# Keys into their slot, transposed in place, and half of wq kept on the chip: two attention and feed-forward layers at decode

## The chip, the core and the metric

The kernel runs on one core of a Trainium2 chip. The metric is the device time of the program in microseconds (us). The engines are called by their short names: PE is TensorE, DVE VectorE, ACT ScalarE, POOL GpSimd, and SP is the engine that issues the loads here. "PEld" is the loading of a weight into the matrix array, which overlaps the products.

## The reference, cut to what matters

One token for each of 8 sequences goes through the same pair of blocks twice: attention over a cache, then a feed-forward network, each behind a layer norm and added to the residual.

```python
B, Sq, D = 8, 1, 512;  Hq, Hkv, Sk, Dh = 32, 8, 8192, 128;  F = 1792
def A(x):                       # x is normalized
    q = (x @ wq)                # 512 x 4096, 32 heads of 128
    scores = q . k * Dh**-0.5   # 4 query heads share one of 8 key heads
    p = softmax(scores)         # over 8192 positions
    return (p @ v) @ wo         # 4096 x 512
def Bf(x):
    return silu(x @ w1) @ w2
x = x + A(norm(x));  x = x + Bf(norm(x))
x = x + A(norm(x));  x = x + Bf(norm(x))
```

All data are bf16. The two caches hold 134 MB each (8 sequences x 8 heads x 8192 x 128), and both layers read them. The kernel reads the keys once, because a sequence's keys stay on the chip from the first layer to the second, and reads the values twice.

## The kernel before

**Units and passes.** The work is cut into units: one layer, one sequence b, one key head g, that is 128 units. There are nine passes (the loop at L909). Pass b = -1 has the eight first-layer units of sequence 0. Pass b = 0 to 6 mixes the second layer of sequence b with the first layer of sequence b+1, alternating; pass 7 has the second layer of the last sequence alone. The second layer of a sequence can start when all its first-layer units have gone through the output projection, the feed-forward block and the next norm. To have something to do over that chain, the values of the last `N_DEF` = 3 second-layer units of a pass are held back and done at the beginning of the next pass (`held`).

**One unit.** `keys` makes p: `expand` (L651) and `spread` (L658) lay the four query heads out as a block-diagonal weight `bd`; `score` (L673) does 64 products, each with 128 columns of keys as the weight; then come the maximum over the unit (`mx` on DVE, `mall` on POOL), the subtraction, the exponential on ACT, a rearrangement through PE (`swap`, L708) and the copy back, with sum and reciprocal beside it. `values` (L755) does 64 products with V as the weight. For a first-layer unit the result goes on through `out_proj_a` with its piece of wo.

**Keys.** In the first layer a head of keys (2 MB) arrives in two halves in the ring (`load_k`, L375). `turns` (L617) transposes it in four pieces with DVE's transpose of 32 x 32 blocks of 32-bit words (two bf16 at a time) from the ring into the head's slot in `kts`, which has eight slots of 2 MB. The second layer of the same sequence uses the slot again; the next sequence's transposes wait for its scores (`scored`). On the way the transposes also set the order of words in a row: from (c4, f, j) to (f, c4, i), so that the 128 columns of one weight lie 4 bytes apart (L674).

**The ring.** `ring` has `N_CELL` = 11 cells of 0.5 MB. Halves of keys and of V take two neighbouring cells, a quarter of half of wq one, a head's piece of wo one. `queries` (L569) loads its half of wq as four cells in every pass, for the first norm and for each sequence; all four have to be there before its products start, and all four are given back after them.

**The order of the work.** All loads are issued by SP, one after the other in the order in which the program lists them (`advance` puts the keys of a unit ahead of the V of the unit before it). SP waits in front of a load until what it overwrites has been read, and everything behind it waits too. What each engine does in which order, and which ring cell a load takes, is settled beforehand by a planner (`Plan`, L134): it steps through the program with fixed durations for each piece of work (for example `T_TURN` for a transpose) and serves, on each engine, the ready piece with the lowest priority number. On the chip each engine then runs its list strictly in order.

**Norms.** `norm_nodes` (L395) sums x and its squares over the partitions with products (L404, L409), makes mean and variance with three small DVE operations (L415, L420, L428), the inverse root on POOL (L433), and applies them (L438). `ffn_nodes` (L456) follows with up, tanh, gate and down. w1 and w2 stay on the chip; `load_ffn` (L864) loads them in the middle of the first pass (L942).

Of the kernel before, what the change touches and what calls it, by code (L numbers as in the profile page):

```python
# [7 lines left out]
DH = 128  # L8
SM_SCALE = DH ** -0.5
LN_EPS = 1e-5  # L10

N_CELL = 11
N_SC = 3
N_P = 3
N_DEF = 3
N_OT = 2
N_BD = 2
T_TURN = 1.2
# [115 lines left out]
class Plan:  # L134
# [3 lines left out]
    RATE = {1: 2.57, 2: 2.51}  # L138
    LAND = 2.0
    HOP = 0.07  # L140
# [107 lines left out]
def _build(ctx, nc, A_x, A_k_cache, A_v_cache, A_wq, A_wo, B_w1, B_w2, out):  # L248
# [22 lines left out]
    kts = sb([128, G * SLOT], BF16, "kts")  # L271
    w1_sb = sb([128, KT, F], BF16, "w1")
    w2_sb = sb([128, FT, D], BF16, "w2")
    ident = sb([128, 128], BF16, "ident")
    ones = sb([128, 1], BF16, "ones")
    sel = sb([128, 4, 4, 32], BF16, "sel")
    sel2 = sb([128, 4, 4, 32], BF16, "sel2")
    mask = sb([128, 4], BF16, "mask")
    expo = sb([128, 8], FP32, "expo")
# [6 lines left out]
    negm = sb([128, 8], FP32, "negm")  # L286
# [18 lines left out]
    ksem = [DmaCounter(syn.new_sem(f"kt{i}")) for i in range(2)]  # L305
    rsem = [DmaCounter(syn.new_sem(f"ring{i}")) for i in range(N_CELL)]
    wsem = {n: DmaCounter(syn.new_sem(f"w_{n}")) for n in ("w1", "w2", "x")}
# [67 lines left out]
    def load_k(b, g, half):  # L375
        src = A_k_cache[b, g].rearrange("(p hh y) d -> hh p (y d)", p=128, hh=2)
        return load_cells(f"k{b}.{g}.{half}", 2, [(lambda buf: buf, src[half])])
# [17 lines left out]
    def norm_nodes(tag, prio, b0, nb, deps):  # L395

        st = MI[:, 480:480 + nb]
# [3 lines left out]
        def stats():  # L401
            steps = []
            for kt in range(KT):
                steps.append(lambda kt=kt: pe.matmul(  # L404
                    st, ones[:, 0:1].to_broadcast([128, 128]), xs[:, bs, kt], start=(kt == 0), stop=(kt == KT - 1)))
            for j in range(nb):
                for kt in range(KT):
                    col = xs[:, b0 + j, kt:kt + 1]
                    steps.append(lambda kt=kt, j=j, col=col: pe.matmul(  # L409
                        sq[:, j:j + 1], col.to_broadcast([128, 128]), col,  # L410
                        start=(kt == 0), stop=(kt == KT - 1)))
            mms(steps, reads=[res("ones"), res("xs")], writes=[res("misc")])

        def mean():
            op(dve, lambda: dve.tensor_scalar(negm[:, 0:nb], st, -1.0 / D, None, op0=ALU.mult),  # L415
               reads=[res("misc")], writes=[res("negm")])

        def vari():
            if nb == 1:
                op(dve, lambda: dve.tensor_scalar(  # L420
                    var[:, 0:1], st, negm[:, 0:1], sq, op0=ALU.mult, op1=ALU.add),
                    reads=[res("misc"), res("negm")], writes=[res("var")])
            else:
                op(dve, lambda: dve.tensor_tensor(var[:, 0:nb], st, negm[:, 0:nb], ALU.mult),
                   reads=[res("misc"), res("negm")], writes=[res("var")])
                op(dve, lambda: dve.tensor_tensor(var[:, 0:nb], sq, var[:, 0:nb], ALU.add),
                   reads=[res("misc"), res("var")], writes=[res("var")])
            op(dve, lambda: dve.tensor_scalar(  # L428
                var[:, 0:nb], var[:, 0:nb], 1.0 / D, LN_EPS, op0=ALU.mult, op1=ALU.add),
                reads=[res("var")], writes=[res("var")])  # L430
# [5 lines left out]
        def apply():  # L436
            if nb == 1:
                op(dve, lambda: dve.tensor_scalar(  # L438
                    xn[:, b0, :], xs[:, b0, :], negm[:, 0:1], rstd[:, 0:1], op0=ALU.add, op1=ALU.mult),
                    reads=[res("xs"), res("negm"), res("rstd")], writes=[res("xn")])  # L440
            else:
                nm = negm[:, 0:nb].unsqueeze(2).to_broadcast([128, nb, KT])
                rs = rstd[:, 0:nb].unsqueeze(2).to_broadcast([128, nb, KT])
                op(dve, lambda: dve.tensor_tensor(big_x, xs[:, bs, :], nm, ALU.add),
                   reads=[res("xs"), res("negm")], writes=[res("ring", 1)])
                op(dve, lambda: dve.tensor_tensor(xn[:, bs, :], big_x, rs, ALU.mult),
                   reads=[res("ring", 1), res("rstd")], writes=[res("xn")])

        a = plan.add(f"{tag}.stats", "PE", 0.3 + 0.2 * nb, stats, prio, deps)
        m = plan.add(f"{tag}.mean", "DVE", 0.18, mean, prio, [a])  # L450
        v = plan.add(f"{tag}.var", "DVE", 0.45, vari, prio, [m])
        r = plan.add(f"{tag}.root", "POOL", 0.6, root, prio, [v])
# [53 lines left out]
    st6 = negm[0:NB, 0:6]  # L506
# [3 lines left out]
    def consts():  # L510
        op(pool, lambda: pool.memset(ones[:, :], 1.0), writes=[res("ones")])
# [4 lines left out]
        iv = ident[:, :].rearrange("p (f j e) -> p f e j", f=2, e=2)  # L516
        sv = sel[:, :, :, :].rearrange("p (f e) a j -> p f e a j", f=2)
        for a in range(4):
            op(pool, lambda a=a: pool.tensor_copy(sv[:, :, :, a, :], iv), reads=[res("ident")], writes=[res("sel")])
            op(pool, lambda a=a: pool.tensor_copy(  # L520
                sel2[:, :, a, :], ident[:, :].rearrange("p (dd j) -> p j dd", j=4)),
                reads=[res("ident")], writes=[res("sel2")])
        op(pool, lambda: pool.memset(expo[:, :], -0.5), writes=[res("expo")])
# [7 lines left out]
    def first_norm():  # L531
        op(dve, lambda: dve.bn_stats(st6, xr), reads=[last], writes=[res("negm")])
        op(dve, lambda: dve.bn_aggr(mv, st6), reads=[res("negm")], writes=[res("var")])
        op(dve, lambda: dve.tensor_scalar(mv[:, 1:2], mv[:, 1:2], LN_EPS, None, op0=ALU.add),
           reads=[res("var")], writes=[res("var")])
# [28 lines left out]
    f4 = plan.add("f.turn", "PE", 0.5, first_turn, -5, [f3])  # L564
# [4 lines left out]
    def queries(tag, prio, half, b0, nb, deps):  # L569

        wn = [load_wq(half, kt) for kt in range(KT)]
        out_n = {}
        last = []
        for g0, g1 in ((4 * half, 4 * half + 1), (4 * half + 1, 4 * half + 4)):
# [3 lines left out]
            def mul(g0=g0, nh=nh, qp=qp):  # L578
                steps = []
                for h in range(nh):  # L580
                    c = (R * g0 + h) * DH - GR * half
                    for kt in range(KT):
                        steps.append(lambda h=h, kt=kt, c=c: pe.matmul(  # L583
                            qp[:, h * nb:(h + 1) * nb], gran(wn[kt].give)[:, c:c + DH], xn[:, b0:b0 + nb, kt],
                            start=(kt == 0), stop=(kt == KT - 1)))
                mms(steps, reads=[r for w in wn for r in cells_of(w)] + [res("xn")], writes=[res("misc")])

            def copy(g0=g0, g1=g1, qp=qp):
                hd = slice(R * g0, R * g1)
                if nb == 1:  # L590
                    op(dve, lambda: dve.tensor_copy(qtb[:, hd], qp), reads=[res("misc")],
                       writes=[res("qtb", g) for g in range(g0, g1)])
                else:
                    op(dve, lambda: dve.tensor_copy(qab[:, :, hd], qp.rearrange("p (h b) -> p b h", b=nb)),
                       reads=[res("misc")], writes=[res("qab", g) for g in range(g0, g1)])

            m = plan.add(f"{tag}.q{g0}", "PE", 0.5 * (g1 - g0), mul, prio, wn + deps + last)
            last = [plan.add(f"{tag}.qc{g0}", "DVE", 0.17, copy, prio, [m])]
            for g in range(g0, g1):
                out_n[g] = last[0]  # L600
        for w in wn:
            frees(m, w)
        return out_n

# [12 lines left out]
    def turns(b, g):  # L617

        tn = []
        new = slot(g).bitcast(U32).rearrange("p (q ck f c4 i) -> p q ck c4 f i", q=4, f=2, i=32, c4=4)  # L620
        for half in range(2):
            kn = load_k(b, g, half)
            for c in range(2):
                def turn(kn=kn, c=c, q=2 * half + c):
                    raw = gran(kn.give, 2).bitcast(U32).rearrange(
                        "p (q ck c4 f j) -> p q ck c4 f j", q=2, c4=4, f=2, j=32)
                    op(dve, lambda: dve.transpose(new[:, q], raw[:, c]), reads=cells_of(kn),  # L627
                       writes=[res("kt", g)], add=(q > 0))
                tn.append(plan.add(f"t{b}.{g}.{2 * half + c}", "DVE", T_TURN, turn, count[0] + 0.5,
                                   [kn] + scored.get(g, []) + tn[-1:]))  # L630
            frees(tn[-1], kn)
        kept[b, g] = tn

    def keys(layer, b, g, q_dep, late=None):
# [3 lines left out]
        pr = u  # L638
# [33 lines left out]
        for q in range(4):  # L672
            def score(q=q):  # L673
                kv = slot(g).rearrange("p (ck f n e) -> p ck f e n", f=2, ck=NCG, e=2)  # L674
# [80 lines left out]
    def values(h, wo=None):  # L755
# [34 lines left out]
        else:  # L790
# [6 lines left out]
            def spread():  # L797
                steps = [lambda j=j: pe.matmul(  # L798
                    ot[:, 8 + R * j:8 + R * j + R], sel2[:, j].rearrange("p a k -> p (a k)"), attna[:, hd],
                    start=True, stop=True) for j in range(R)]  # L800
                mms(steps, reads=[res("sel2"), res("attna", g)], writes=[res("ot", o)])
# [78 lines left out]
    def load_wo_all():  # L880
        for i in range(2):
            n = plan.load(f"woall{i}", 4, None, scored[2 * i], ring=False)

            def emit(i=i):
                dma(sp, slot(2 * i).rearrange("p (h d) -> p h d", h=16), wo_v[:, 16 * i:16 * i + 16, :], ksem[i],
# [23 lines left out]
    for b in range(-1, NB):  # L909
        ready = None  # L910
        prio = count[0] - 4
        if b >= 0:
# [4 lines left out]
            for k, h in enumerate(held):  # L917
                if k == 1:
                    second_q.update(queries(f"c{b}", prio, 0, b, 1, [ready]))
                values(h)  # L920
                ends.append(h)
# [4 lines left out]
        def advance(unit):  # L926
            while unit not in made:
                k = todo.pop(0)
                layer, kb, g = k
                if layer == 0:  # L930
                    turns(kb, g)
                    if kb == 0 and g % 4 == 0:
                        first_q.update(queries("f", count[0] - 5, g // 4, 0, NB, [f5]))
                    made[k] = keys(0, kb, g, first_q[g])
                else:
                    if g % 4 == 0 and g >= (4 if held else 0):
# [83 lines left out]
```

## Time and profile before

| what | value |
|---|---|
| median of 3 runs | 1231.23 us (1230.66 to 1232.52) |
| the profiled execution | 1229.31 us |
| its span, from the first to the last instruction | 1227.8 us |
| busy: PE, PEld, DVE, ACT, POOL | 56%, 51%, 44%, 9%, 10% |
| bytes moved, mean rate over the span | 485.00 MB, 395 GB/s |
| V loads, each from issue to landing (median) | 256 of 1 MB, 10.0 us |
| key loads | 128 of 1 MB, 10.1 us |
| wq loads | 72 of 0.5 MB, 11.0 us |
| wo loads | 64 of 0.5 MB, 10.4 us; at the end 2 of 2 MB, 16.5 us |
| transposes of keys (L627) | 256, 310.8 us of DVE |
| products with V (L775), products of the scores (L678) | 8192 of each |

The page cuts the span into 40 slices and gives, for each, the busy share of every engine and the rate of the transfers. A row of a group reads: line, engine, operation, out<-in, shapes, count | busy us, mean ns of one | idle time of the engine just before them, and what ended it. The time of a load from issue to landing includes the loads queued ahead of it. A window's row has its bounds, its length, busy us and count for PE, PEld, DVE, ACT and POOL, the granted clock, the busy share of the transfers, and GB/s.

### The profile page before, as it was taken

How to read it: one execution, taken by the hardware profiler on the slowest of the kernel's cores; microseconds unless marked ns; L12 is line 12 of the kernel's file. 1: busy time of each engine (PE TensorE's matmuls, PEld its weight loads, DVE VectorE, ACT ScalarE, POOL GpSimd, SP SyncE). 2: the span in 40 equal slices, each digit the busy share in tenths (PEclk: the TensorE clock that was granted, in tenths of full speed). 3: DMA queues.
4: the chain of work that ended last, by engine and by line, in shares of the span. 5: the costliest groups of instructions: out<-in, count | busy, mean ns of one | idle time of the engine just before them, and what ended most of it. 6: DMA issues, size and time to landing. Idle time of an engine off the chain costs nothing.

```text
span 1227.8 us, 48979 instructions
## 1 busy us (share of the span) xinstructions
PE 683.5 (56%) x22688; PEld 627.0 (51%) x22688; DVE 536.5 (44%) x1236; ACT 108.9 (9%) x330; POOL 117.1 (10%) x295
## 2 busy tenths in 40 slices
PE   3334656565565655646556564656556555565665
PEld 2333545465454654546455464545545455454554
DVE  5533445614364254633446334461536515454221
ACT  0000000101011010100101000010101100011000
POOL 1000100101011010101001010010101101010110
DMA  9999699999999999999999999999999999999994
GB/s 371 416 405 417 272 403 419 416 390 417 409 417 408 385 419 416 415 404 367 417 399 417 415 393 417 406 403 373 420 416 403 412 368 408 412 417 401 383 370 186
DMA packets 81580, 485.00 MB, mean 395 GB/s; under 512 B 8400, under 2 KB 14304, under 8 KB 32224
## 3 DMA queue, kind: packets, MB, share of 16 engines
q1 hardware_dynamic: 81376, 481.87, 96.8%
q8 instruction: 178, 2.92, 0.9%
q14 instruction: 26, 0.21, 0.0%
HBM read 481.83 MB, written 0.01 MB: 392 GB/s over the span
## 4 chain that ended last, share of the span: by engine, by line
DMA 40%; issue 21%; PE 18%; DVE 15%; POOL 2%; SPq 2%; ACT 1%; POOLq 0%; DVEq 0%
DMA ring<-in_A_v_cache_dram 28%; DVE kts L627 9%; DMA ring<-in_A_k_cache_dram 9%; PE ot L775 6%; PE sc L678 5%; DMA ring<-in_A_wq_dram 3%; SPq L327 2%; PE misc L583 2%; DVE sc L700 2%; DVE small L690 1%; PE misc L485 1%; PE misc L467 1%; POOL small L695 1%; PE sc L715 1%; DVE small L725 1%
## 5 line engine op out<-in xcount | busy, mean ns | idle before, releaser
L775 PE MATMUL ot<-p,ring 128*128 128x4 bf16 x8192 | 283.2, 167 | 241.1 <-DMA ring<-in_A_v_cache_dram 202.1
L775 PEld LDWEIGHTS ot<-p,ring 128*128 128x128 bf16 x8192 | 252.7, 104 | 260.7 <-DMA ring<-in_A_v_cache_dram 214.6
L627 DVE STREAM_TRANSPOSE kts<-ring 128x1024 uint32<-128x1024 uint32 x256 | 310.8, 1228 | 43.7 <-DMA ring<-in_A_k_cache_dram 43.1
L678 PE MATMUL sc<-bd,kts 128*128 128x16 bf16 x8192 | 275.6, 175 | 88.1 <-issue 59.0
L678 PEld LDWEIGHTS sc<-bd,kts 128*128 128x128 bf16 x8192 | 247.9, 104 | 99.3 <-issue 64.5
L690 DVE TENSOR_REDUCE small<-sc 128x4 f32<-128x256 f32 x128 | 53.9, 421 | 237.5 <-PE sc L678 237.5
L695 POOL PARTITION_ALL_REDUCE small<-small x128 | 47.6, 372 | 726.1 <-DVE small L690 681.8
L705 ACT ACTIVATE expd<-sc 128x256 bf16<-128x256 f32 x128 | 48.9, 382 | 556.8 <-DVE sc L700 550.8
L715 PE MATMUL sc<-expd,ident 128*32 128x64 bf16 x2048 | 54.0, 239 | 48.1 <-ACT expd L705 35.7
L730 POOL PARTITION_ALL_REDUCE small<-small x128 | 55.0, 430 | 236.1 <-DVE small L725 202.2
L700 DVE TENSOR_TENSOR sc<-sc,small 128x256 f32<-128x256 f32 x128 | 54.0, 422 | 31.6 <-POOL small L695 31.6
L583 PE MATMUL misc<-xn,ring 128*128 128x1 bf16 (+1 forms) x1152 | 36.5, 166 | 49.6 <-DMA ring<-in_A_wq_dram 32.0
L725 DVE TENSOR_REDUCE small<-expd 128x4 f32<-128x256 bf16 x128 | 51.2, 400 | 23.0 <-ACT expd L705 23.0
L715 PEld LDWEIGHTS sc<-expd,ident 128*32 128x32 bf16 x2048 | 31.9, 118 | 56.7 <-ACT expd L705 43.3
L583 PEld LDWEIGHTS misc<-xn,ring 128*128 128x128 bf16 x1152 | 33.9, 104 | 52.3 <-issue 48.1
L721 ACT ACTIVATE p<-sc 128x256 bf16<-128x256 f32 x128 | 49.0, 383 | 114.7 <-PE sc L715 114.7
L827 PE MATMUL yt<-z,ring 128*128 128x4 bf16 x1024 | 37.0, 167 | 39.5 <-DVE z L805 26.6
L827 PEld LDWEIGHTS yt<-z,ring 128*128 128x128 bf16 x1024 | 32.9, 104 | 44.2 <-issue 43.0
L805 DVE TENSOR_TENSOR z<-ot,small 128x16 bf16<-128x16 f32 x64 | 10.5, 164 | 82.4 <-PE ot L798 82.4
L794 ACT ACTIVATE attna<-ot 128x4 bf16<-128x4 f32 x64 | 11.1, 173 | 362.8 <-PE ot L775 362.8
L786 DVE TENSOR_TENSOR qab<-ot,small 128x4 bf16<-128x4 f32 x64 | 10.2, 160 | 74.0 <-PE ot L775 74.0
L662 DVE TENSOR_TENSOR bd<-qx,mask 128x64 bf16<-128x64 f32 x128 | 27.6, 216 | 19.4 <-PE qx L654 19.4
(64 smaller groups left out, 250.4 us busy)
## 6 DMA issues: line engine op xcount, KB each, us to landing
ring<-in_A_v_cache_dram SPq DMA_DIRECT2D x256, 1024.0 KB, 10.0
ring<-in_A_k_cache_dram SPq DMA_DIRECT2D x128, 1024.0 KB, 10.1
ring<-in_A_wq_dram SPq DMA_DIRECT2D x72, 512.0 KB, 11.0
ring<-in_A_wo_dram SPq DMA_DIRECT2D x64, 512.0 KB, 10.4
kts<-in_A_wo_dram SPq DMA_DIRECT2D x2, 2048.0 KB, 16.5
w<-in_B_w_dram SPq DMA_DIRECT2D x2, 1792.0 KB, 15.3
ring<-in_A_x_dram SPq DMA_DIRECT2D x1, 8.0 KB
out_dram<-ring SPq DMA_DIRECT2D x1, 8.0 KB
```

Source lines behind the costliest of these rows:

```text
L583: steps.append(lambda h=h, kt=kt, c=c: pe.matmul(qp[:, h * nb:(h + 1) * nb], gran(wn[kt].give)[:, c:c + DH], xn[:, b0:b0 + nb, kt], start= ...
L627: op(dve, lambda: dve.transpose(new[:, q], raw[:, c]), reads=cells_of(kn), writes=[res("kt", g)], add=(q > 0))
L678: steps.append(lambda cg=cg, fe=fe: pe.matmul(sc[:, 16 * cg:16 * cg + 16], kv[:, cg, fe // 2, fe % 2], bd[:, 16 * fe:16 * fe + 16], start= ...
L690: op(dve, lambda: dve.tensor_reduce(mxp[sm], sv.rearrange("p (k h) -> p h k", h=R), AX.X, ALU.max), reads=[res(*scr)], writes=[res("mxp", ...
L695: op(pool, lambda: pool.partition_all_reduce(mxa[sm], mxp[sm], 128, bass.bass_isa.ReduceOp.max), reads=[res("mxp", sm)], writes=[res("mxa" ...
L700: op(dve, lambda: dve.tensor_tensor(v, v, mxa[sm].unsqueeze(1).to_broadcast([128, NCH, R]), ALU.subtract), reads=[res("mxa", sm)], writes= ...
L715: steps.append(lambda c4=c4, P=P: pe.matmul(new[32 * P:32 * P + 32, c4], ident[:, 32 * c4:32 * c4 + 32], src[:, P], start=True, stop=True))
L721: op(act, lambda: act.activation(pt[:, :], sc[:, 256:512], ACT.Copy), reads=[res(*scr)], writes=[res("p", sm)])
L725: op(dve, lambda: dve.tensor_reduce(ssm[sm], pe_out[:, :].rearrange("p (k h) -> p h k", h=R), AX.X, ALU.add), reads=[res("expd")], writes= ...
L730: op(pool, lambda: pool.partition_all_reduce(ssa[sm], ssm[sm], 128, bass.bass_isa.ReduceOp.add), reads=[res("ssm", sm)], writes=[res("ssa" ...
L775: steps.append(lambda x=x, k=k: pe.matmul(ot[:, 0:R], vt[:, x, :], pt[:, k:k + R], start=(P == 0 and x == 0), stop=(P == 3 and x == NCG - 1)))
L827: steps.append(lambda j=j, dt=dt: pe.matmul(YT[:, dt * R:(dt + 1) * R], w[:, j, dt * 128:(dt + 1) * 128], zt[:, R * j:R * j + R], start=(g ...
```

## The change

Keys are no longer loaded into the ring. One load of 2 MB per head goes straight to the slot in `kts`, and waits there for the scores of the slot's last user. The four transposes work in place: each takes words 8 bytes apart (f is now the innermost index of a row), 1024 words of each partition, and writes the transposed block where it read it. All of them wait for the whole head. The 128 columns of a score weight then lie 8 bytes apart.

The ring shrinks from 11 to 7 cells. In the room that this frees, `wq0`, half of wq (the queries of heads 0 to 3) stays on the chip; it is loaded once. The other half still comes through the ring in every pass, but its four cells are used and given back one by one (`queries_1`). `N_DEF` goes from 3 to 4. Keys are listed two units ahead instead of one, except at the start of a pass. `load_ffn` moves from the middle of the first pass to its end. The work of the chain between passes gets the lowest priority numbers (`FIRST`). In the norm, the sums give the negative mean directly (weights of -1/D), eps is added by two products, the squares use x/D made by ACT, and two small DVE operations go. `sel2` is dropped, since `sel` now has its layout. Some of the planner's durations change too.

```diff
-N_CELL = 11
+N_CELL = 7
-N_DEF = 3
+N_DEF = 4
-T_TURN = 1.2
+T_TURN = 1.23
+FIRST = -1000000
...
-    RATE = {1: 2.57, 2: 2.51}
+    RATE = {1: 2.57, 2: 2.51, 4: 2.48}
-    HOP = 0.07
+    HOP = 0.1
...
+    wq0 = sb([128, KT, GR], BF16, "wq0")
...
-    def load_k(b, g, half):
-        src = A_k_cache[b, g].rearrange("(p hh y) d -> hh p (y d)", p=128, hh=2)
-        return load_cells(f"k{b}.{g}.{half}", 2, [(lambda buf: buf, src[half])])
+    def load_k(b, g):
+        n = plan.load(f"k{b}.{g}", 4, lambda: dma(
+            sp, slot(g), A_k_cache[b, g].rearrange("(p y) d -> p (y d)", p=128), ksem[g], writes=[res("kt", g)]),
+            scored.get(g, []), ring=False)
+        return n
...
     def turns(b, g):
+        kn = load_k(b, g)
         tn = []
-        new = slot(g).bitcast(U32).rearrange("p (q ck f c4 i) -> p q ck c4 f i", q=4, f=2, i=32, c4=4)
-        for half in range(2):
-            kn = load_k(b, g, half)
-            for c in range(2):
-                def turn(kn=kn, c=c, q=2 * half + c):
-                    raw = gran(kn.give, 2).bitcast(U32).rearrange(
-                        "p (q ck c4 f j) -> p q ck c4 f j", q=2, c4=4, f=2, j=32)
-                    op(dve, lambda: dve.transpose(new[:, q], raw[:, c]), reads=cells_of(kn),
-                       writes=[res("kt", g)], add=(q > 0))
+        for q in range(4):
+            def turn(q=q):
+                v = slot(g).bitcast(U32).rearrange("p (q n f) -> p q f n", q=4, f=2)[:, q]
+                op(dve, lambda: dve.transpose(v, v), reads=[], writes=[res("kt", g)], add=(q > 0))
...
-                kv = slot(g).rearrange("p (ck f n e) -> p ck f e n", f=2, ck=NCG, e=2)
+                kv = slot(g).rearrange("p (ck n f e) -> p ck f e n", f=2, ck=NCG, e=2)
...
+    def queries_1(tag, prio, b0, nb, deps):
+        qp = MI[:, 0:16 * nb]
+        last = []
+        for kt in range(KT):
+            wn = load_wq(1, kt)
+            def mul(kt=kt, wn=wn):
+                ...
+            last = [plan.add(f"{tag}.r{kt}", "PE", 0.5, mul, prio, [wn] + deps + last)]
+            frees(last[0], wn)
...
-            for k, h in enumerate(held):
-                if k == 1:
-                    second_q.update(queries(f"c{b}", prio, 0, b, 1, [ready]))
+            second_q.update(queries_0(f"c{b}", prio, b, 1, [ready]))
+            for h in held:
                 values(h)
...
-            advance(vs[min(i + 1, len(vs) - 1)])
-            if b < 0 and i == 4:
-                load_ffn()
+            advance(vs[min(i + (1 if i == 0 and b >= 0 else 2), len(vs) - 1)])
...
+        if b < 0:
+            load_ffn()
```

## The prediction

> **What bounds the kernel now.** I read the page from its second part, because this is one long stream of loads: 485 MB are read and 8 KB written.
>
> ```profile
> DMA  9999699999999999999999999999999999999994
> GB/s 371 416 405 417 272 403 419 416 390 417 409 417 408 385 419 416 415 404 367 417 399 417 415 393 417 406 403 373 420 416 403 412 368 408 412 417 401 383 370 186
> ...
> q1 hardware_dynamic: 81376, 481.87, 96.8%
> ```
>
> The transfer engines are full in 38 of 40 slices, and a full slice moves 417 GB/s. TensorE is busy for 56% of the span, VectorE for 44%. So time is bytes plus holes: 485.00 MB at 417 GB/s are 1163 us, the span is 1227.8 us, and 65 us are holes. The table by 10 us windows tells where (the last column is GB/s):
>
> ```profile
> 120.00:130.00 10.00, 4.48 (x144) 4.18 (x143) 2.10 (x10) 0.18 (x1) 1.14 (x2) 1.00 0.45 184
> 130.00:140.00 10.00, 6.22 (x217) 5.80 (x215) 4.27 (x13) 0.89 (x3) 1.20 (x3) 1.00 0.72 270
> 140.00:150.00 10.00, 7.66 (x276) 7.40 (x276) 4.88 (x11) 0.62 (x2) 0.80 (x2) 1.00 0.92 354
> ...
> 410.00:420.00 10.00, 7.93 (x287) 7.79 (x284) 1.93 (x10) 0.00 (x0) 0.56 (x1) 1.00 0.83 315
> ...
> 1210.00:1220.00 10.00, 5.10 (x167) 4.67 (x164) 1.31 (x9) 0.00 (x0) 1.69 (x1) 1.00 0.13 50
> ```
>
> A window at r GB/s lost 10 x (417 - r)/417 us. The first change of pass (120 to 150 us) lost 5.6 + 3.5 + 1.5 = 10.6 us; the seven others, as at 410 us, 1.7 to 3.1 us each, 17.4 us; the start 3.6 us; the tail after the last load 8.8 + 7.8 = 16.6 us; the rest, 16.5 us, is thin. Next, what holds the load queue (waits of SP: total, times, longest):
>
> ```profile
> SPq L89 <- PE ot L775: 429.3, 186, 8.2
> SPq L89 <- DVE kts L627: 262.8, 101, 7.8
> SPq L89 <- PE misc L583: 85.3, 13, 13.5
> ```
>
> SP waits all the time for ring cells: from the products with V, from the transposes of keys, from the query products. It costs little as long as enough is in flight. How much is enough is in the chain of waits (start, duration), at loads of 1 MB issued into a nearly empty queue:
>
> ```profile
> 131.88 5.09 DMA ring<-in_A_k_cache_dram
> ...
> 1147.29 5.03 DMA ring<-in_A_v_cache_dram
> ```
>
> Such a load lands 5.1 us after its issue; 2.5 us of it are wire time (1.05 MB at 417 GB/s), 2.6 us are fixed. Last, the groups that the change touches:
>
> ```profile
> L627 DVE STREAM_TRANSPOSE kts<-ring 128x1024 uint32<-128x1024 uint32 x256 | 310.8, 1228 | 43.7 <-DMA ring<-in_A_k_cache_dram 43.1
> L775 PE MATMUL ot<-p,ring 128*128 128x4 bf16 x8192 | 283.2, 167 | 241.1 <-DMA ring<-in_A_v_cache_dram 202.1
> L678 PEld LDWEIGHTS sc<-bd,kts 128*128 128x128 bf16 x8192 | 247.9, 104 | 99.3 <-issue 64.5
> L725 DVE TENSOR_REDUCE small<-expd 128x4 f32<-128x256 bf16 x128 | 51.2, 400 | 23.0 <-ACT expd L705 23.0
> ```
>
> [...] The trace has one such case: L725 reads bf16 in steps of 8 bytes (h inside k, reduced over k), 256 elements in 400 ns, 1.56 ns each even with all its fixed cost in it[...]; a write, and TensorE's weight load, no row shows.
>
> **The change, part by part.**
>
> *Half of wq resident.* Before, each of 9 passes loads both halves, 72 loads of 0.524 MB; after, 4 once and 4 in each pass, 40 loads. 32 x 0.524 = 16.8 MB leave the queue. They lie in stretches where the wire is the limit: 16.8 / 0.417 = -40.2 us. That is the change's main term, and holds as long as the wire stays full.
>
> *Keys straight to their slot.* 128 ring loads of 1 MB become 64 loads of 2 MB into kts; same bytes. SP no longer waits for L627 (262.8 us of waits that the wire hid); it waits instead for the scores of the slot's last user, with every later load of V, wo and wq behind it. By the order of the instructions those scores stand well ahead except for head 0 of each pass, right behind the chain of feed-forward and queries. A transpose waits for 2 MB rather than 1: 2.5 us later. From key landing to p: 4 x 1.23 + scores 64 x 28 ns = 1.8, softmax with its hops about 3, sharing of VectorE 1 to 2: some 11 to 12 us. The key's V starts landing 12.5 us (head 0) to 20 us after it, since keys are now loaded two units ahead. Hidden, with about 1 us to spare at head 0 and 3 us at head 7 (5.0 + 2 x 6.3 - 2.5 = 15.1 us).
>
> *Transposes in place, steps of 8 bytes.* I take 1.23 us[...]. [...]
>
> *Weights of the scores in steps of 8 bytes instead of 4.* I take 104 ns with a new one every 28 ns (48 in 1.36 us), as now; the bad end is double, 8192 x 28 = +229 us of TensorE.
>
> *Ring of 11 cells to 7.* V, wo and the rest of wq share 3.5 MB. By the cells that the planner gives out, before, each load had 3.5 MB or more between it and the load whose cells it takes; after, mostly 3.5 to 4.5 where keys lie between, but 2.0 through the held units and 1.5 at three V halves of heads 6 and 7. The working: consumption is 32 products, 1.2 us, then 5.2 us from issue to landing with the wait's hop: 6.4 us. With m MB between, the wire has 2.5 x (m + 1): 7.5 us at 2.0 (1.1 us to spare), 6.25 us at 1.5 (a hole of 0.15 us, plus whatever delays TensorE). Delays are real: up and down (1.65 us each) and the query products (0.6 and 1.4 us) stand between the held V products. I put 1.6 us on the three tight halves (scores of the last head stand between their products, 2 x 0.45 us) and leave the change of pass at the 2.5 us that it loses now (17.4 / 7): net +1.6 us for each of 8 passes, +13 us. From both sides: -8 us (changes of pass lose 1.5 us, tight halves nothing) and +40 us.
>
> *Changes of pass.* No wq load comes between norm and first query (the 85.3 us of waits on L583 become few), four held units (20 us of wire) instead of three (15 us) cover the chain. From the last V product to the scores of head 0 the first change shows in the chain 12.1 us (117.99 to 130.13) to the first query products, and then 1.4 + 0.3 + 1.8 = 3.5: 15.6 us. Each norm loses two small VectorE operations (L415 159 ns, L428 154 ns, with hops 0.4 us) and gains six products; its new ACT step runs beside the sums: -0.3 us, twice. The cover, with V of head 0, is 25 us: no wait for the key of head 0. In the first change nothing is held, but w1 and w2 are now loaded there: 8.8 us, and V of head 0 5.0 us. Key 0 is issued 1.2 + 15.6 - 0.6 = 16.2 us after the last landing and lands 2.6 + 5.0 us later, at 23.8 us; a full wire would have it at 18.8. So 5.0 us are lost instead of 10.6: -5.6 us.
>
> *Tail and constants.* The last norm has eight columns: 12 products more, one VectorE operation less, nothing. sel and sel2 merge: nothing, POOL is idle.
>
> Sum on the profiled execution: 1227.8 - 40.2 - 5.6 + 13 = 1195 us of span. The metric is 1.5 us above its span there (1229.31), and the median of the runs 1.9 us above that: **1198 us**.
>
> **Rivals.** (1) *The short ring starves the wire.* The gain is 36 us over 8 changes of pass and the passes before them; from 4 us more per pass than I put (say eight holes of half a microsecond) the kernel is slower than before. For it: idle DMA time needs only 1.1 us of delay at 2.0 MB. Against it: TensorE is half idle, and the order of its instructions serves V early. A mild form, 2 us more per pass, gives 1214 us; the strong one, 6 us, 1246 us. (2) *Steps of 8 bytes are dear.* On TensorE double weight loads take the dense stretch (key, wo and V of one head, 11.3 us of wire) from 7.0 to 10.6 us of TensorE, and delays of 1 us pass the slack everywhere: about 1230 us. [...] Against both: L725. (3) *Better than summed:* the changes of pass hold nothing up, 1178 us. (4) *The gain is hidden anyway*, because something but the wire binds: against it the 417 GB/s in nearly all slices.
>
> **How the numbers follow.** Mine (1186 to 1212 us) 0.60; better (3) 0.10; ring mild 0.08, strong 0.12; steps 0.08, nearly all of it slower; (4) 0.02. The range 1178 to 1240 us leaves out half the better case, the upper half of the strong ring and the dear VectorE step. Under 0.2%, about 2.5 us, a measurement can't be told from no change. Faster 0.79, the same 0.03, slower 0.18.
>
> **What would show it.** About 468.2 MB and a mean of 395 GB/s or more; L627 x256 at 1.23 us; LDWEIGHTS of the scores at 104 ns; SP waiting mostly for L775, and for L678 only at the first change; a hole of some 5 us near the first change with w1 and w2 in it, and 2 to 4 us at each later one. Wrong if full windows stay under 417 GB/s in the middle of passes, if L627 or the score weights got longer, or if SP stands at key 0 in every pass.

## The result and the profile after

The changed kernel takes 1249.5 us (median of 4 runs, 1240.9 to 1250.4) against 1231.0 us before: 1.0135 times the time by the means, 95% interval 1.0089 to 1.0182. It is slower, where the forecast was 1198 us. The profiled execution took 1240.85 us, its span is 1239.1 us; it is the fastest of the four, the others took 1249.5 to 1250.4 us.

Parts 2 and 3 of the page of the changed kernel, the rate of the transfers in 40 slices and the load queue:

```profile
DMA  9999899999998999999999999998999989999995
GB/s 375 417 408 348 327 417 417 344 349 411 406 422 324 360 417 412 417 350 370 403 418 376 352 369 410 419 364 318 410 410 414 364 334 418 420 414 340 330 342 198
...
DMA packets 67756, 468.22 MB, mean 378 GB/s; under 512 B 6864, under 2 KB 12768, under 8 KB 26592
...
q1 hardware_dynamic: 67552, 465.09, 94.5%
```

The bytes went as expected: 468.22 MB instead of 485.00, and full slices still move 417 GB/s or so. But in each pass of four to five slices two or three now lie under 380, down to 318, where before the dip at a change of pass was mostly one slice, at 367 to 393 (272 at the first change). 468.22 MB at 417 GB/s are 1122.8 us; 116.3 us of the span are holes, against 64.7 before. So 40.2 us of wire time left, and 51.6 us of holes came.

The table by windows of 10 us (the last column is GB/s) tells where:

```profile
120.00:130.00 10.00, 7.98 (x254) 7.74 (x254) 2.08 (x9) 0.20 (x1) 0.71 (x2) 1.00 0.29 116
130.00:140.00 10.00, 5.99 (x194) 5.52 (x191) 4.44 (x11) 1.54 (x4) 1.45 (x4) 1.00 0.98 381
...
230.00:240.00 10.00, 4.94 (x164) 4.70 (x164) 3.28 (x10) 0.94 (x3) 0.80 (x2) 1.00 0.86 299
240.00:250.00 10.00, 3.52 (x108) 3.22 (x109) 0.17 (x1) 0.17 (x1) 0.00 (x0) 1.00 0.91 335
250.00:260.00 10.00, 7.25 (x247) 6.87 (x245) 1.42 (x7) 0.56 (x3) 0.60 (x1) 1.00 0.97 376
260.00:270.00 10.00, 6.77 (x223) 6.45 (x220) 1.68 (x8) 0.20 (x1) 0.55 (x1) 1.00 0.96 358
270.00:280.00 10.00, 7.03 (x233) 6.68 (x231) 2.88 (x10) 1.15 (x3) 1.20 (x3) 1.00 0.83 315
```

One change of pass, 230 to 280 us, loses (417 x 5 - 299 - 335 - 376 - 358 - 315) / 41.7 = 9.6 us. These 50 us are the end of one pass, with no key to load until 272.7 us, and the held units of the next. In 240 to 250 us VectorE, ScalarE and POOL do next to nothing and TensorE is busy for a third: everything waits for V while the wire has room. PE's part of the timeline there (start, duration, what, idle time before it and its releaser) and the chain of waits in the same stretch:

```profile
241.13 1.01 PE L809 MATMUL ot<-p,ring 128*128 128x4 bf16 x32 [4.02 <-DMA ring<-in_A_v_cache_dram]
...
249.34 1.02 PE L809 MATMUL ot<-p,ring 128*128 128x4 bf16 x32 [4.71 <-DMA ring<-in_A_v_cache_dram]
...
254.29 1.01 PE L809 MATMUL ot<-p,ring 128*128 128x4 bf16 x32 [1.05 <-DMA ring<-in_A_v_cache_dram]
255.17 1.63 PE L482 MATMUL misc<-xn,w 128*128 128x1 bf16 x56
257.87 1.01 PE L809 MATMUL ot<-p,ring 128*128 128x4 bf16 x32 [1.07 <-DMA ring<-in_A_v_cache_dram]
```

```profile
233.74 7.34 DMA ring<-in_A_v_cache_dram
...
243.62 1.03 PE ot L809 x32
...
244.71 9.54 DMA ring<-in_A_v_cache_dram
254.25 0.05 issue
254.29 1.03 PE ot L809 x32
...
255.38 8.13 DMA ring<-in_A_v_cache_dram
```

That is a closed loop: V lands, 32 products use it, SP issues the next half into its cells at once, and that half takes 7.3 to 9.5 us to land. SP's own waits (total, times, longest) say the same:

```profile
SPq L91 <- PE ot L809: 824.9, 233, 20.0
SPq L91 <- PE sc L712: 87.6, 15, 14.8
```

The wait for the products with V nearly doubled (429.3 before); the transposes (262.8) are gone from the list. Last, the groups:

```profile
L809 PE MATMUL ot<-p,ring 128*128 128x4 bf16 x8192 | 279.9, 167 | 249.8 <-DMA ring<-in_A_v_cache_dram 216.5
...
L712 PEld LDWEIGHTS sc<-bd,kts 128*128 128x128 bf16 x8192 | 303.6, 117 | 87.8 <-issue 41.5
L664 DVE STREAM_TRANSPOSE kts<-kts 128x1024 uint32<-128x1024 uint32 x256 | 310.4, 1227 | 39.2 <-DMA kts<-in_A_k_cache_dram 39.2
```

The transposes in steps of 8 bytes cost what they did (1227 ns). The score weights do not: 117 ns instead of 104, and from the starts in the trace one every 33 ns (median) instead of 27.

### The profile page after: what moved, and what is told of

Read it like the earlier page. It is cut to its first block, busy times and chain, and to the rows that moved or that the text cites. A ratio compares the mean times of both kernels' runs of the same rounds, so it can differ in the third digit from the quotient of the medians.

```text
span 1239.1 us, 48861 instructions
## 1 busy us (share of the span) xinstructions
PE 732.7 (59%) x22804; PEld 680.4 (55%) x22804; DVE 530.5 (43%) x1194; ACT 113.7 (9%) x347; POOL 116.8 (9%) x295
## 2 busy tenths in 40 slices
DMA packets 67756, 468.22 MB, mean 378 GB/s; under 512 B 6864, under 2 KB 12768, under 8 KB 26592
## 4 chain that ended last, share of the span: by engine, by line
DMA 57%; PE 22%; issue 12%; DVE 6%; POOL 1%; SPq 1%; ACT 0%; POOLq 0%; DVEq 0%
DMA ring<-in_A_v_cache_dram 45%; PE sc L712 9%; PE ot L809 8%; DMA kts<-in_A_k_cache_dram 7%; DVE kts L664 4%; DMA ring<-in_A_wq_dram 4%; DMA w<-in_B_w_dram 1%; PE misc L612 1%; PE sc L749 1%; PE qx L688 1%; PE yt L861 1%; DVE sc L734 1%; SPq L330 1%; PE misc L635 1%; DVE small L724 1%
## 5 line engine op out<-in xcount | busy, mean ns | idle before, releaser
L809 PE MATMUL ot<-p,ring 128*128 128x4 bf16 x8192 | 279.9, 167 | 249.8 <-DMA ring<-in_A_v_cache_dram 216.5
L712 PE MATMUL sc<-bd,kts 128*128 128x16 bf16 x8192 | 329.4, 179 | 79.7 <-issue 39.1
L712 PEld LDWEIGHTS sc<-bd,kts 128*128 128x128 bf16 x8192 | 303.6, 117 | 87.8 <-issue 41.5
L664 DVE STREAM_TRANSPOSE kts<-kts 128x1024 uint32<-128x1024 uint32 x256 | 310.4, 1227 | 39.2 <-DMA kts<-in_A_k_cache_dram 39.2
L688 PE MATMUL qx<-qab,sel 128*128 128x4 bf16 x256 | 16.8, 170 | 29.3 <-DVE bd L696 28.9
L447 POOL TENSOR_TENSOR rstd<-var,expo 128x1 f32<-128x1 f32 (+1 forms) x17 | 10.9, 642 | 216.6 <-DVE var L437 191.5
## 6 DMA issues: line engine op xcount, KB each, us to landing
wq<-in_A_wq_dram SPq DMA_DIRECT2D x4, 512.0 KB, 10.9
```

The lines of the kernel that those rows point to most:

```text
L664: op(dve, lambda: dve.transpose(v, v), reads=[], writes=[res("kt", g)], add=(q > 0))
L712: steps.append(lambda cg=cg, fe=fe: pe.matmul(sc[:, 16 * cg:16 * cg + 16], kv[:, cg, fe // 2, fe % 2], bd[:, 16 * fe:16 * fe + 16], start= ...
L809: steps.append(lambda x=x, k=k: pe.matmul(ot[:, 0:R], vt[:, x, :], pt[:, k:k + R], start=(P == 0 and x == 0), stop=(P == 3 and x == NCG - 1)))
```

## The experiments

Two theories stood after the result. **R**: the ring of 7 cells lets too little be in flight, and the wire starves. **W**: the slower score weights (TensorE is busy with the scores for 329.4 us instead of 275.6) delay the products with V, so that cells come back late. Each run is compared with runs of the kernel before on the same chip (medians 1228.5 to 1230.5 us); runs from different chips are compared through these ratios.

### Weights, ring, and both

```diff
 # the first: score weights read as before (wrongly ordered keys)
-kv = slot(g).rearrange("p (ck n f e) -> p ck f e n", f=2, ck=NCG, e=2)
+kv = slot(g).rearrange("p (ck f n e) -> p ck f e n", f=2, ck=NCG, e=2)
 # the second: 10 cells in the room of w2
-N_CELL = 7
+N_CELL = 10
-    w2_sb = sb([128, FT, D], BF16, "w2")
+    w2_sb = w1_sb[:, :, :].rearrange("p a b -> p (a b)").rearrange("p (f d) -> p f d", f=FT)
```

The third has both edits; the fourth puts the new `kv` line into the kernel before.

> The changed kernel, but the score products read their 128 columns 4 bytes apart as the kernel before did; the transposes still write them 8 bytes apart, so the scores are formed from wrongly ordered keys and the output differs. Theory R (the ring of 7 cells starves the wire): score weights are back at 27 ns apart instead of 34, 55 us of TensorE are gone, but the time stays at 1230 to 1247 us. Theory W (the slower weights hold V up, and with it the ring): 1190 to 1208 us.

> The changed kernel with 10 ring cells instead of 7. The room comes from leaving w2 out: its products read the tile of w1, so the feed-forward result differs, and one load of 1.8 MB less (at most 4 us). Score weights stay at 34 ns. Theory R: most of the 54 us of new holes close, 1180 to 1200 us. Theory W: 1230 to 1245 us.

> Both edits at once: 10 ring cells with w2 left out, and score weights in steps of 4 bytes on wrongly ordered keys. Either theory: 1172 to 1192 us, that is what the removed bytes promised. If it is still above 1215 us, neither ring nor weights is the cause, but the order of the work.

> The kernel before, with the score weights read in steps of 8 bytes (from keys that lie 4 bytes apart, so the scores are formed from wrongly ordered keys). Its ring is deep. The weights should be 34 ns apart and TensorE 57 us busier. Theory R: hidden under the loads, 1229 to 1240 us. Theory W: 1250 to 1285 us.

| run | median us | ratio to before (95%) | score weights | holes at 417 GB/s, us |
|---|---|---|---|---|
| weights back | 1243.3 | 1.0104 (1.0067 to 1.0141) | 104 ns | 118 |
| 10 cells | 1183.6 | 0.9607 (0.9578 to 0.9637) | 117 ns | 63 |
| both | 1183.4 | 0.9604 (0.9572 to 0.9636) | 104 ns | 63 |
| before, new weights | 1231.9 | 1.0013 (0.9992 to 1.0033) | 118 ns | 70 |

The groups of the score weights, of the run with the weights put back and of the kernel before with the new ones:

```profile
L712 PEld LDWEIGHTS sc<-bd,kts 128*128 128x128 bf16 x8192 | 249.4, 104 | 97.0 <-issue 53.3
```

```profile
L678 PEld LDWEIGHTS sc<-bd,kts 128*128 128x128 bf16 x8192 | 301.9, 118 | 80.8 <-issue 48.0
```

The price of the weights moves with the step of the read and nothing else, and it is paid in TensorE's idle time: with 7 cells, with 10 and in the kernel before, the time is the same with and without it, within the intervals. W falls. With three more cells (and without the load of w2, for which the next section has the control) the new holes are gone: 63 us, as before the change. The page of the run with 10 cells, and SP's waits in it:

```profile
GB/s 370 419 419 353 322 416 417 402 375 424 416 422 404 374 420 422 416 401 395 419 415 409 406 355 418 416 405 387 414 416 415 403 372 422 411 408 411 357 347 190
```

```profile
SPq L91 <- PE ot L809: 510.8, 153, 12.9
SPq L91 <- PE sc L712: 275.4, 42, 19.8
```

The dips are back to one per change of pass, except at the first (353 and 322) and in the last pass. SP now stands before keys, waiting for scores (275.4 us). Mostly this costs little, because the wire has work queued meanwhile. It does cost something before the key of head 0: at all seven changes of pass that have keys to load SP waits there for the scores of head 0. By the landings in the trace the holes in front of these keys are 10.9 us at the first change and 1.3 to 3.7 us at each of the six others, 23.5 us together.

### How many cells, and the control

```diff
 # w2 left out as above
-N_CELL = 7
+N_CELL = 8          # and, as the control, 7
```

> As the run with 10 cells (w2 left out, its products read the tile of w1), but 8 cells: one cell more than the changed kernel. Theory R with the slack as the measure: three whole V halves and the wo cell fit beside one free cell, so about half of the 60 us come back: 1205 to 1228 us. If it were only that w2 was left out that made the run with 10 cells fast, 8 cells would be as fast: 1180 to 1190 us.

> The control for the runs with 8 and 10 cells: w2 left out in the same way (its products read the tile of w1), but the ring at its 7 cells. Theory R: 1236 to 1250 us, as the changed kernel less at most 4 us. If leaving w2 out made those runs fast: 1180 to 1200 us.

With w2 left out, 7 cells take 1240.7 us (1.0094, 1.0062 to 1.0126), 8 cells 1192.3 (0.9692, 0.9669 to 0.9715), 10 cells 1183.6. So leaving w2 out is not what made those runs fast; and the eighth cell alone is worth 48 us, the next two 9 (49 and 10 by the ratios). I had expected half the loss back from it; the step is far steeper. The pages with 7 cells and with 8, w2 left out in both:

```profile
GB/s 371 419 407 293 379 414 423 349 330 415 408 419 316 355 418 420 409 346 358 415 418 372 331 395 411 416 367 331 421 407 417 355 334 411 417 400 357 300 337 201
```

```profile
GB/s 371 420 417 342 341 418 418 405 382 419 418 421 390 363 419 421 418 390 377 421 419 411 372 388 413 415 413 351 417 416 419 396 375 401 416 417 389 334 346 190
```

What the planner gives out goes with it. For each V load that takes cells used before I counted the MB that are loaded between it and the load whose cells it takes:

```
cells          V loads   2.0 MB or less   2.5 or less
before, 11     256        2                3
after, 7       253       93              107
8              253       18               48
10             252        3               20
```

The number of loads with 2.0 MB or less between follows the loss: 93, 18, 3 loads; 1240.7, 1192.3, 1183.6 us. With another number of cells the planner also lays out the work anew, so the order of the products is not held fixed in these runs. But the place of the holes speaks for the ring. I give each load the time from the landing before it to its own, less its own wire time at 417 GB/s: in the changed kernel 74.6 us of idle wire stand in front of the 93 tight halves and 4.0 us in front of the 163 other V halves. With 8 cells it is 9.2 us for the 18, with 10 cells 2.5 us for the 3; in the kernel before all 256 V halves together have 29.9 us.

### Smaller pieces of V in the same 7 cells

The quarters: V in four loads of one cell, each freed after its 16 products. The pairs: the same loads, but two wait for each other and are freed together.

```diff
-        src = A_v_cache[b, g].rearrange("(p hh y) d -> hh p (y d)", p=128, hh=2)
-        return load_cells(f"v{b}.{g}.{half}", 2, [(lambda buf: buf, src[half])])
+        src = A_v_cache[b, g].rearrange("(p hh y) d -> hh p (y d)", p=128, hh=4)
+        return load_cells(f"v{b}.{g}.{part}", 1, [(lambda buf: buf, src[part])])
...
-            if P % 2 == 0:
-                vn = load_v(b, g, P // 2)
+            vn = load_v(b, g, P)
...
-            if P % 2:
-                frees(n, vn)
+            frees(n, vn)
 # the pairs, beside it
+            if P % 2 == 0:
+                pair = [load_v(b, g, P), load_v(b, g, P + 1)]
...
-                mms(steps, reads=cells_of(vn) + ...
+                mms(steps, reads=cells_of(pair[0]) + cells_of(pair[1]) + ...
```

> The changed kernel, its 7 cells, 34 ns weights and everything else kept, but V is loaded in four loads of 0.5 MB and one cell each, freed after 16 products, instead of two of 1 MB and two cells freed after 32. The result is the reference's. Theory R: the ring holds 3.0 to 3.5 MB in flight instead of 2.0 to 2.5, most holes close: 1190 to 1212 us. If what counts is the number of loads in flight and not the bytes, it gains as much or more; if smaller loads each pay the fixed time, nothing is gained: 1235 to 1255 us.

> The kernel before with V in four loads of 0.5 MB and one cell each. Its ring of 11 cells has 3.5 MB or more between a load and the one whose cells it takes. Theory R: nothing to gain, 1226 to 1236 us. If smaller loads are dearer on the wire (128 rows of 4 KB instead of 8 KB): 1240 us and more; if they are better by themselves, below 1220 us, and the run with quarters in 7 cells says less about the ring.

> As the run with V in quarters, 7 cells, but two quarters wait for each other and are given back together, after 32 products: the cells need not be neighbours, but space comes back in pieces of 1 MB as in the changed kernel. If the quarters helped because space comes back earlier: 1230 to 1250 us. If they helped because a pair of V needs no two neighbouring cells any more (7 cells hold wo and three V halves only when the single cell lies well): 1195 to 1212 us.

> The changed kernel, 7 cells, V in quarters only where the ring runs short: first-layer heads 6 and 7, second-layer heads 4 to 7, and the last pass; halves elsewhere. The result is the reference's. If quarters everywhere cost some wire rate (their full slices moved 413 instead of 418 GB/s) and the holes are only at the ends of passes: 1186 to 1196 us, faster than quarters everywhere. If halves also starve in the middle of passes: 1200 to 1220 us.

| run | median us | ratio to before (95%) | holes at 417 GB/s, us |
|---|---|---|---|
| quarters, 7 cells | 1198.8 | 0.9744 (0.9721 to 0.9767) | 75 |
| kernel before, quarters | 1227.0 | 0.9980 (0.9966 to 0.9994) | 60 |
| quarters freed in pairs | 1235.0 | 1.0048 (1.0030 to 1.0065) | 114 |
| quarters where the ring runs short | 1207.6 | 0.9829 (0.9798 to 0.9860) | 83 |

The pages of the quarters and of the pairs:

```profile
GB/s 371 415 413 392 307 414 413 403 384 406 412 413 400 362 415 418 402 404 379 412 413 413 393 388 415 414 399 371 403 412 411 397 375 415 417 408 402 312 356 193
```

```profile
GB/s 371 416 411 353 331 403 414 369 363 402 408 402 364 355 400 414 410 353 357 404 414 383 358 374 397 414 377 352 399 405 415 364 331 410 416 412 361 316 348 195
```

With the same 7 cells and the slow weights, the quarters take 48 us off the changed kernel (0.9744 against 1.0135); where the ring is deep they gain 0.2%. That small number hides two effects that nearly cancel, as the page of the kernel before with quarters shows:

```profile
GB/s 368 412 401 410 331 403 410 410 408 400 411 411 399 408 403 412 406 398 409 406 412 394 408 405 410 404 405 407 411 410 400 404 409 370 412 410 402 408 374 195
```

No slice is over 412 GB/s, where the halves reach 416 to 420, and the dips at most changes of pass are nearly gone. So quarters close holes with 11 cells too, and pay for it in rate.

It is not that single cells need no neighbours, nor the number and size of the loads: the pairs share both with the quarters, but gain only about 11 us over the changed kernel (1.0048 against 1.0135) and keep dips of 316 to 374. What counts is that V is used and its space given back in pieces of 0.5 MB. The pairs take back two things at once, the start of the products when the first quarter is there and the return of the cells after 16 of them; which of the two is worth more, no run separates. The count of MB between loads does not carry over to pairs: only 26 of their 506 loads have 2.0 MB or less, and 114 us are holes.

Quarters only in the tight places were slower than quarters everywhere, the second of the two outcomes that I had named. But the cause named with it, halves that starve in the middle of passes, is not what the trace shows. Windows of that run, from two changes of pass and from the middle of the pass between them:

```profile
400.00:410.00 10.00, 7.08 (x242) 7.02 (x242) 1.74 (x8) 0.00 (x0) 0.39 (x1) 1.00 0.56 202
...
440.00:450.00 10.00, 4.74 (x160) 4.23 (x157) 4.46 (x12) 1.48 (x5) 1.23 (x3) 1.00 1.00 417
...
690.00:700.00 10.00, 8.75 (x290) 8.45 (x287) 2.69 (x11) 0.77 (x2) 0.83 (x2) 1.00 0.58 202
```

The largest holes of its changes of pass after the first, 3.1 to 6.1 us each and 25.5 us in six, stand in front of the first V half of head 0 of the second layer, right behind the held units, with 1.5 to 2.0 MB between it and the load whose cells it takes. I had left that place in halves; no run has it in quarters and the middle of the passes in halves.

The quarters in 7 cells are the version that beats both kernels with every product in place, 2.6% under the one before. Most of their full slices move 411 to 415 GB/s. Whether the size of the load or its rows of 4 KB instead of 8 KB lowers the rate, no run separates.

### Residency taken away, and the feed-forward loads alone

```diff
 # changed kernel, both halves of wq through the ring
-N_CELL = 7
+N_CELL = 11
-    wq0 = sb([128, KT, GR], BF16, "wq0")
...
+        wn = [load_wq(0, kt) for kt in range(KT)]
-                            qp[:, h * nb:(h + 1) * nb], wq0[:, kt, c:c + DH], xn[:, b0:b0 + nb, kt],
+                            qp[:, h * nb:(h + 1) * nb], gran(wn[kt].give)[:, c:c + DH], xn[:, b0:b0 + nb, kt],
 # kernel before, load_ffn from the middle of the first pass to its end
-            if b < 0 and i == 4:
-                load_ffn()
...
+        if b < 0:
+            load_ffn()
```

In the first of these two runs the query products of heads 0 to 3 also stand behind the first held unit, as in the kernel before.

> The changed kernel without the resident half of wq: both halves come through the ring in every pass as before, 485.0 MB, and the 16 KB go back to the ring, which has 11 cells. Keys still go straight to their slot and are transposed in place. If the whole gain of the change is in the removed bytes and the whole loss in the ring: as the kernel before, 1222 to 1236 us. If the keys' direct way costs (waits on scores): above 1240 us. If it gains by itself: below 1215 us.

> The kernel before with one part of the change: w1 and w2 are loaded at the end of the first pass instead of its middle. They then run on the wire while the first change of pass computes. As worked out in the prediction for the changed kernel (10.6 us of hole become 5.0): 1223 to 1227 us. If the wire simply idles later: 1229 to 1233 us.

Without residency, at 485.0 MB, the changed kernel takes 1211.0 us (0.9843, 0.9824 to 0.9862), 18 us under the one before with as many cells; its holes are 46 us instead of 65. The outcome that I had named first was no difference; it was the third, a gain by itself. Moving the feed-forward loads alone gives 1222.7 us (0.9955, 0.9941 to 0.9970), -5.8 us. If the parts add, the other 12 us come from the keys' direct way, the two units of lookahead, the fourth held unit, the second half of wq used and given back piece by piece, the shorter norm and the priorities of the chain together; which of them, no run separates. SP's waits without residency show the queue standing before keys for 282.4 us, at little cost:

```profile
SPq L91 <- PE ot L811: 594.5, 183, 8.3
SPq L91 <- PE sc L714: 282.4, 35, 15.9
```

## Why the prediction was wrong, point by point

**Right: what bounds the kernel, and the bytes.** 468.22 MB as said, 40.2 us of wire time less. Whether they turn into time depends on the ring: the run with 10 cells is 46.9 us under the kernel before. But against the run without residency, which has all else of the change and 11 cells, it is only 27 us faster for 18.6 MB less (w2 included), which are 44.7 us at 417 GB/s. It has 17 us of holes more. The keys of head 0 account for them: in front of these stand 23.5 us over the seven changes of pass, against 4.5 us without residency. 5 of them are in the first change (11.4 us lost against 6.5, by the windows; the load of w2 is missing there as cover). At the six others SP waits there for the scores of head 0, which it does not without residency; why, no run separates, since ring, query order and wq loads differ together. The prediction had "no wait for the key of head 0".

**Wrong: the ring's term.** This is the step that failed. The prediction put +13 us on "ring of 11 cells to 7", with -8 and +40 as its ends; from 7 to 10 cells the runs measure 57 us (1240.7 against 1183.6, w2 left out in both). The mechanism was named, as rival 1, and its strong form (1246 us, 0.12) is what came; its size was off in three places.

First, the 6.4 us from a landing to the next landing in the same cells. Its 5.1 us from issue to landing came from loads issued into a nearly empty queue. Worked out from the issues and landings in the trace of the changed kernel, by how many loads were still in flight when a V half was issued:

```
in flight   V halves   issue to landing   landing after the one before it
                       median us          median us (2.5 = no hole)
1           21          6.07              3.42
2           93          7.19              2.77
3           78          9.99              2.48
```

(The other 64 of the 256 had four or more in flight, or none.)

With two in flight a half lands 7.2 us after its issue and still leaves a hole, though it was issued 4.15 us (median) before the load ahead of it landed; by the prediction's 5.1 us from issue to landing, 2.6 us would have been enough. Sorted by this lead over the load ahead, a half lands 3.1 us after that load when the lead was 3 to 4 us (33 halves), 2.7 us after it at 4 to 5 us (34 halves), and only from 5 us on 2.5 us after it, with no hole (medians). So the loop is 1.2 + 7.2 = 8.4 us and not 6.4, and at 2.0 MB between (7.5 us of wire) it leaves 0.9 us of hole in each round of three loads instead of 1.1 us to spare; 0.3 us per load is what the row with two in flight has (2.77 - 2.48). Why the lead has to be so long stays open. The sixteen parts of a load finish at different times, but the time from the first to the last is 1.44, 1.96 and 2.71 us with one, two and three in flight, and with three there is no hole.

Second, what the tight loads cost. Their number was about right: the prediction knew the three halves at 1.5 MB and the held units at 2.0, some 11 per pass, and the planner gives 93 of 253 V halves 2.0 MB or less. But it gave the three 1.6 us together and the others nothing beyond the 2.5 us of today's change of pass. The 74.6 us in front of the 93 are some 9 us per pass, 0.8 us each. Also "before, 3.5 MB or more" was read too coarsely: 19 of 256 had 3.0 or less.

Third, a hole there delays itself: the products wait for V (4.0 and 4.7 us in the timeline above), so the next cells come back later.

That the span with 10 cells (1181.8 us) is the prediction's sum without the ring's term (1182 us) is luck: it holds some 12 us of gain that the prediction did not have, the 23.5 us before the keys of head 0, of which it had only the 5 us of the first change, and one load less. In rival 1, "the gain is 36 us" should read 33 (40.2 + 5.6 - 13); nothing hangs on it.

**Wrong in size, harmless: the score weights.** I took 104 ns and the same spacing, with double as the bad end; both were assumptions, since no row of the trace before has a weight read in such steps. It is 117 ns and 33 ns apart, and 54 of the 229 us of the bad end, a quarter. The rival that called it dear was right that it costs something, at a quarter of its price, and wrong on the effect: 54 us of TensorE vanish in its idle time, with 7 cells, with 10 and in the kernel before.

**Right: the transposes.** 1227 ns in steps of 8 bytes, read and write, against 1228 ns before. L725 had pointed there for the read, with 256 elements in 400 ns; that the write would keep pace was an assumption, since no row before showed it.

**Partly right: the first change of pass.** The prediction had 5.0 us lost instead of 10.6. In the changed kernel its windows (110 to 140 us) lose 0.8 + 7.2 + 0.9 = 8.9 us: the chain of waits shows `down` standing for w2 until 120.09 us and key 0 issued only at 129.32, after the scores. The wait that the prediction put at nothing is this one: it took w1 and w2 as cover for a chain that itself needs them. Key 0 was issued 19.3 us after the last landing of the pass's V (110.06), not 16.2, and landed 8.7 us later, not 7.6.

```profile
103.65 16.39 DMA w<-in_B_w_dram
120.04 0.05 issue
120.09 1.67 PE misc L500 x56
...
129.29 0.03 issue
129.32 0.33 SPq L330
129.65 0.05 issue
```

The part done alone in the kernel before gives -5.8 us, near the predicted -5.6. But there the chain of waits stands for a load of wq until 121.93 us, so the number agrees and the path does not:

```profile
111.75 10.18 DMA ring<-in_A_wq_dram
```

**Left out: a gain in the rest of the change.** "Hidden" was the value of the keys' direct way; with 11 cells the changed kernel without residency is 18 us faster, 12 of them not from the feed-forward loads. The prediction looked for what the new waits would cost and found that they are covered, which holds except before the keys of head 0, but gave no value to what was removed: 1 MB pieces of keys no longer take two of the ring's cells until they are transposed. That this is where the gain is from is an inference.

The parts do not simply add: -18 us for everything but the residency with 11 cells, some -27 us more for residency with 10 cells (w2 left out), +57 us for going on to 7 cells, and a last 5 to 9 us, the difference between the control with 7 cells and the changed kernel, of which some 4 us are the load of w2; the intervals of these two overlap. The upper end that the ring's term was given, +40, is itself below the 57 us.

## What to carry to other kernels

In a kernel like this one, bound by the stream of loads, room for bytes in flight is the resource: price a smaller buffer by the loop from landing to landing in the same space, with the landing time measured at the depth that the new kernel will have, not in an empty queue, and count from the planner how many loads fall under it. Find out which loads the holes stand in front of before choosing what to mend. Here the limit is a cliff: one cell of 0.5 MB was worth 48 us and the next two 9. Smaller pieces, given back earlier, bought almost the same as more room (48 us) without a byte of it. An engine with idle time took 54 us more work for nothing.

## What the runs showed of the hardware that was not expected

- A 128-column bf16 weight read in steps of 8 bytes loads in 117 ns and one every 33 ns, against 104 and 27 ns in steps of 4 bytes (8192 loads each, in both kernels).
- A transpose of 32-bit words on VectorE, in place, reading and writing every other word, takes 1227 ns for 1024 columns, as with adjacent words (1228 ns).
- The time from issue to landing of 1 MB grows with the queue beyond the wire time of what is ahead: 5.1 us in a nearly empty queue, 7.2 us with two in flight, of which the load ahead explains 4.15 + 2.5 = 6.65. In the changed kernel a V half landed without a hole only when it was issued some 5 us before the load ahead of it landed.
- V in loads of 0.5 MB with rows of 4 KB, instead of 1 MB with rows of 8 KB: in the kernel before, no slice moves more than 412 GB/s, where full slices moved 416 to 420.
